# A decode-attention kernel whose output weights partly travel by five DMA engines: 320 instead of 480 rows of `wo` on that way, the rest of the quarter five rows to a partition

## The chip, the core and the metric

The kernel runs on one core of a Trainium2 chip. The metric is the time of one execution on the device in microseconds (us). Four runs of the kernel before took 189.28, 189.11, 190.93 and 194.01 us; their median is 190.1 us. The execution that was profiled is the one of 189.28 us; its profiled span is 187.5 us, which leaves 1.8 us around the span.

## The reference, cut to what matters

Attention of 4 new tokens in each of 8 sequences against a cache of 2048 keys, with 32 query heads that share 8 key/value heads, followed by the output projection. All arrays are bf16.

```python
B, Sq, D = 8, 4, 512
Hq, Hkv, Sk, Dh = 32, 8, 2048, 128
q = (x @ wq).reshape(B, Sq, Hq, Dh)                    # wq: 512 x 4096
scores = einsum("bhqd,bhkd->bhqk", q, k) * Dh ** -0.5  # k, v repeated 4 times over heads
p = softmax(scores)
o = einsum("bhqk,bhkd->bhqd", p, v)
out = o.reshape(B, Sq, Hq * Dh) @ wo                   # wo: 4096 x 512
```

Keys and values are 32 MB (2^20 bytes each) apiece, `wq` and `wo` 4 MB apiece: 72 MB are read from HBM once, and 32 KB are written.

## The kernel before, in words

**Units.** The 8 key/value heads are taken in 4 pairs and the 8 sequences one by one, which makes 32 units. A unit has 1 MB of keys and 1 MB of values, each in one tile of 128 partitions x 8192 bytes (`load_k` L108, `load_v` L118). The main loop (L405) runs over the units: it transposes the keys of unit n on TensorE (L198), copies them from PSUM on VectorE (L200), makes the scores of unit n-1 (L261), the exponentials (L272), and, two units behind, the values product (L321). Seven key tiles and six value tiles are in rotation.

**The order of the transfers.** All loads are issued by SyncE, whose queue is in the order of the list built in L148 to L158: keys of unit 0, all of `wq`, `x`, then eight small pieces of `wo` (`wo_e`, one after each of the first units), keys and values in turn, and after the values of unit 31 the pieces `wo_n` and `wo_m`. The other three quarters of `wo` follow at the end of the list (L430 to L435) in eight transfers: four of 512 KB and four of 256 KB.

**The first quarter of `wo`.** The first 1024 rows of `wo` belong to head pair 0. They are split three ways by the constants in L51:

```python
NE, WE, WM = 40, 12, 4
assert NE * WE + 128 * WM + 32 == HP * 128
```

- `wo_e`: 40 partitions with 12 rows each, 480 rows. It is loaded by `load_wo_e` (L128) in eight transfers of 5 partitions, 12,288 bytes to a partition. Since a transfer has five partitions, five DMA engines carry it, one partition each.
- `wo_m`: 128 partitions with 4 rows each, 512 rows, in one transfer of 4096 bytes to a partition (L137).
- `wo_n`: 32 partitions with 1 row each, the last 32 rows, in one transfer (L136).

The attention output must lie in the same row order to be multiplied with these pieces. `to_tokens` (L341) transposes the output of the pair to tokens and copies it to `nat_sb` (L355, L356, L359), where gaps are filled with other columns so that 64 partitions can be treated alike; the memset of `wo_e` (L173) has made the unused partitions zero. `to_wo_rows` (L361) transposes it into one slice for each row index (L376, L379, L380) and copies the slices to `oE`, `oM`, `oN` (L381 to L383).

**The projection.** `project` (L385) multiplies one slice with one row set, in two halves of 256 columns, and adds into the PSUM tile `out_ps`. Rows of `wo_e` are used after units 14 to 17, three for each (L439); `wo_m` and `wo_n` after unit 30 (L441); the other three quarters at the end (L445 to L451), pair 3 in the steps in which its 256 KB pieces arrive. Then ScalarE copies the result (L453), and two transfers write it out.

**SyncE's queue.** A transfer is issued only when the one eight places before it has landed (the queue waits show it), so at most eight are under way. The 16 DMA engines each take their share of every transfer in that order.

Of the kernel before, what the change touches and what calls it, by code (L numbers as in the profile page):

```python
# [8 lines left out]
BF16 = mybir.dt.bfloat16  # L9
# [5 lines left out]
def kernel(  # L15
# [9 lines left out]
    nc = tc.nc  # L25

    B, Sq, D = x.shape
# [4 lines left out]
    T = B * Sq  # L32
# [7 lines left out]
    HP = 2 * rep  # L40
# [7 lines left out]
    DH = D // 2  # L48


    NE, WE, WM = 40, 12, 4  # L51
    assert NE * WE + 128 * WM + 32 == HP * 128
    AX = mybir.AxisListType.X
    ADD = mybir.AluOpType.add
    assert Dh == 128 and C == 32 and NQ == 32 and G2 == 4
# [1 line left out]
    const = ctx.enter_context(tc.tile_pool(name="const", bufs=1))  # L57
# [15 lines left out]

    pad0 = const.tile([128, 192], BF16, name="pad0")
    wo_e = const.tile([64, WE, D], BF16, name="wo_e")
    wo_n = const.tile([32, D], BF16, name="wo_n")
    wo_m = const.tile([128, WM, D], BF16, name="wo_m")
    x_sb = const.tile([T, D], BF16, name="x_sb")
    wq_sb = wpool.tile([128, R, HqDh], BF16, tag="w", name="wq_sb")
# [9 lines left out]
    oT = [const.tile([128, HP, len(ps), B, Sq], BF16, name=f"oT{ps[0]}") for ps in groups]  # L89
    out_sb = const.tile([2 * T, DH], BF16, name="out_sb")  # L90
    oP12 = const.tile([128, WR, 2, T], BF16, name="oP12")
    nat_sb = const.tile([2 * T, HP * 128 + 288], BF16, name="nat_sb")
    oP3 = const.tile([128, WR, T], BF16, name="oP3")
    oP = [None, oP12[:, :, 0, :], oP12[:, :, 1, :], oP3[:, :, :]]
    oE = const.tile([64, WE, T], BF16, name="oE")
    oM = const.tile([128, WM, T], BF16, name="oM")
    oN = const.tile([32, T], BF16, name="oN")
    ident = const.tile([128, 128], BF16, name="ident")
    by_q = const.tile([128, HQ], FP32, name="by_q")
    ones = const.tile([128, 128], FP32, name="ones")  # L100
    pad = const.tile([128, 160], BF16, name="pad")
    probs = [const.tile([128, C, 2, HQ], BF16, name=f"probs{i}") for i in range(3)]

    units = [(p, b) for p in range(G2) for b in range(B)]
# [28 lines left out]
        nc.sync.dma_start(wo_e[a : a + 17 : 4, :, :], rows[b : b + 17 : 4, :, :])  # L133

    def load_wo_m():
        nc.sync.dma_start(wo_n[:, :], wo[HP * 128 - 32 : HP * 128, :])  # L136
        nc.sync.dma_start(  # L137
            wo_m[:, :, :], wo[NE * WE : HP * 128 - 32, :].rearrange("(q r) j -> q r j", r=WM)
        )

    def load_wo(p, r0, n):
        rows = wo[p * HP * 128 : (p + 1) * HP * 128, :].rearrange("(q r) j -> q r j", r=WR)
        nc.sync.dma_start(wo_sb[:, p - 1, r0 : r0 + n, :], rows[:, r0 : r0 + n, :])
# [34 lines left out]
    for e in range(2):  # L178
        for g in range(2):
            nc.vector.tensor_copy(  # L180
                out=pick[:, e, g, :], in_=ident[:, :].rearrange("d (k e) -> d e k", e=2)[:, e, :]
            )
    nc.vector.memset(q_bd[:, :, :, :, :, :, :], 0.0)
    for t in probs:
# [3 lines left out]
        out=by_q[:, :], in_=ident4[:, :].rearrange("p (c q) -> p q c", q=HQ), axis=AX, op=ADD  # L188
# [4 lines left out]
    def transpose_part(u, t):  # L193
        kp = psum_k.tile([128, JT, 128], FP32, tag="k", name="kp")
        k4 = ks[u][:, :, :].rearrange("s c d -> s (c d)").bitcast(FP32)
        for j in range(JT):
            w = (t * JT + j) * 128
            nc.tensor.transpose(kp[:, j, :], k4[:, w : w + 128], ident4[:, :])  # L198
        k_t = ktpool.tile([128, JT, 128, 2], BF16, tag="kt", name="kt")
        nc.vector.tensor_copy(  # L200
            out=k_t[:, :, :, :].rearrange("k j s e -> k (j s e)"),
            in_=kp[:, :, :].rearrange("k j s -> k (j s)").bitcast(BF16),
        )
        kt[(u, t)] = k_t
# [9 lines left out]
    for p in range(G2):  # L214
        psq = (psum_t.tile([128, HP, T], FP32, tag="t", name="psq")
               if p % 2 else psum_s.tile([128, HP, T], FP32, tag="s", name="psq"))
        for h in range(HP):
# [10 lines left out]
            out=qT_all[:, p, :, :, :],  # L228
            in_=psq[:, :, :].rearrange("d h (b s) -> d b h s", b=B),
            mul=scale,  # L230
        )
    for pp in range(0, G2, 2):
        for e in range(2):
# [9 lines left out]
            for g in range(2):  # L243
                rows = slice(g * 64, (g + 1) * 64)
                (nc.scalar.copy if g else nc.vector.tensor_copy)(  # L245
                    out=q_bd[rows, pp : pp + 2, e, :, :, g, :].rearrange("d p b g q -> d p (b g) q"),
                    in_=pse[rows, :, :, :, :].rearrange("d p b g q -> d p (b g) q"),
# [68 lines left out]
    def values(u):  # L316
        pr = probs[u % len(probs)]
        o_ps = psum_o.tile([128, NQ], FP32, tag="o", name="o_ps")
        for i in range(C):
            j, t, c = i // 8, i // 2 % 4, i % 2  # L320
            nc.tensor.matmul(  # L321
                o_ps[:, :],
                lhsT=vs[u][:, 2 * (t * JT + j) + c, :],
                rhs=pr[:, i, :, :].rearrange("s g q -> s (g q)"),
                start=(i == 0),
                stop=(i == C - 1),
            )
        o_pss[u] = o_ps
# [10 lines left out]
    nats = {}  # L339

    def to_tokens(n):  # L341
        rows = len(groups[n]) * T
        nat = psum_l.tile([rows, HP, 128], BF16, tag="l", name="nat")
        for h in range(HP):
            nc.tensor.transpose(
                nat[:, h, :], oT[n][:, h, :, :, :].rearrange("d p b s -> d (p b s)"), ident[:, :]
            )
        flat = nat[:, :, :].rearrange("t h d -> t (h d)")
        nats[n] = nat_sb[:rows, : HP * 128 + (n == 0) * 288]
        if n > 0:  # L350
            nc.vector.tensor_copy(out=nats[n][:, :], in_=flat)
            return

        w = 32 * WE
        nc.vector.tensor_copy(out=nats[0][:, :w], in_=flat[:, :w])  # L355
        nc.vector.tensor_copy(  # L356
            out=nats[0][:, w : 2 * w], in_=flat[:, NE // 2 * WE : NE // 2 * WE + w]
        )
        nc.vector.tensor_copy(out=nats[0][:, 2 * w :], in_=flat[:, NE * WE :])  # L359

    def to_wo_rows(n):  # L361
        rows = len(groups[n]) * T
        if n > 0:
            perm = psum_l.tile([128, WR, rows], BF16, tag="l", name="perm")
            by_row = nats[n][:, :].rearrange("t (q r) -> t r q", r=WR)
            for r in range(WR):
                nc.tensor.transpose(perm[:, r, :], by_row[:, r, :], ident[:rows, :rows])
            to = oP3[:, :, :] if n == 2 else oP12[:, :, :, :].rearrange("q r p t -> q r (p t)")
            nc.vector.tensor_copy(out=to, in_=perm[:, :, :])
            return  # L370

        perm = psum_l.tile([128, WE + WM + 1, T], BF16, tag="l", name="perm")
        w = 64 * WE
        by_row = nats[0][:, :w].rearrange("t (q r) -> t r q", r=WE)
        for r in range(WE):
            nc.tensor.transpose(perm[:64, r, :], by_row[:, r, :], ident[:T, :T])  # L376
        by_row = nats[0][:, w : w + 128 * WM].rearrange("t (q r) -> t r q", r=WM)
        for r in range(WM):
            nc.tensor.transpose(perm[:, WE + r, :], by_row[:, r, :], ident[:T, :T])  # L379
        nc.tensor.transpose(perm[:32, WE + WM, :], nats[0][:, w + 128 * WM :], ident[:T, :T])  # L380
        nc.vector.tensor_copy(out=oN[:, :], in_=perm[:32, WE + WM, :])  # L381
        nc.vector.tensor_copy(out=oE[:, :, :], in_=perm[:64, :WE, :])
        nc.vector.tensor_copy(out=oM[:, :, :], in_=perm[:, WE : WE + WM, :])  # L383

    def project(p, r0, n):  # L385

        for r in range(r0, r0 + n):
            if p > 0:
                o, w = oP[p][:, r], wo_sb[:, p - 1, r]
            elif r < WE:  # L390
                o, w = oE[:, r, :], wo_e[:, r]
            elif r < WE + WM:
                o, w = oM[:, r - WE, :], wo_m[:, r - WE]
            else:
                o, w = oN[:, :], wo_n
            for half in range(2):
                nc.tensor.matmul(  # L397
                    out_ps[half * T : (half + 1) * T, :],
                    lhsT=o,
                    rhs=w[:, half * DH : (half + 1) * DH],  # L400
                    start=(p == 0 and r == 0),
                    stop=(p == G2 - 1 and r == WR - 1),
                )

    for n in range(NU + A):  # L405
        w = n - A
        for t in range(2):
            if 0 < n < NU:
                transpose_part(n, t)
        if 0 <= n - 1 < NU:  # L410
            scores(n - 1)
        for t in range(2, 4):
            if 0 < n < NU:
                transpose_part(n, t)
        if w >= 0:
            p, b = units[w]
            if p in (1, 3) and b == 1:
                to_tokens(p // 2)
            values(w)
            if p in (1, 3) and b == 2:  # L420
                to_wo_rows(p // 2)
            if w % 2 == 0:
                norms(w)
            finish(w)
        if 0 <= n - 1 < NU:
            probs_to_keys(n - 1)
        load_ready(min(n + 1, NU), max(w + 1, 0))
        if w == NU - 1 - VB:
            assert not loads
            load_wo(1, 0, 4)  # L430
            load_wo(1, 4, 4)
            load_wo(2, 0, 4)
            load_wo(2, 4, 4)
            for r in range(0, WR, 2):
                load_wo(3, r, 2)  # L435

        if w == 13:
            out_ps = psum_e.tile([2 * T, DH], FP32, tag="e", name="out_ps")
        if 14 <= w < 18:  # L439
            project(0, (w - 14) * 3, 3)  # L440
        if w == NU - 2:  # L441
            project(0, WE, WM + 1)

# [42 lines left out]
```

The softmax here doesn't subtract the row's maximum and nothing guards it: scores larger than these inputs give would overflow.

## Time and profile before

| what | value |
|---|---|
| four runs, us | 189.28, 189.11, 190.93, 194.01 |
| the profiled execution, us | 189.28 |
| its span, us | 187.5 |
| TensorE busy in the span | 145.2 us, 77% |
| VectorE busy | 108.8 us, 58% |
| ScalarE busy | 69.4 us, 37% |
| GpSimd busy | 6.3 us, 3% |
| read from HBM | 75.53 MB (10^6 bytes), 403 GB/s over the span |
| packets of SyncE's DMA queue | 10,880, 96.2% of the time of 16 engines |

How to read the profile: engines are PE (TensorE), PEld (its weight loads), DVE (VectorE), ACT (ScalarE), POOL (GpSimd) and SP (SyncE); a q after the name is the engine's instruction queue. L12 is line 12 of the kernel. A group row has the line, engine and operation, the tiles written and read, the count, then busy microseconds and the mean nanoseconds of one, then the idle time before the group and what ended it. A row of the chain of waits has start, length, and what the end of the execution was waiting for in that stretch. Beside its rows, the trace holds a record for each packet that a DMA engine moved: start, duration, bytes and queue, though not the number of the engine.

### The profile page before, as it was taken

How to read it: one execution, taken by the hardware profiler on the slowest of the kernel's cores; microseconds unless marked ns; L12 is line 12 of the kernel's file. 1: busy time of each engine (PE TensorE's matmuls, PEld its weight loads, DVE VectorE, ACT ScalarE, POOL GpSimd, SP SyncE). 2: the span in 40 equal slices, each digit the busy share in tenths (PEclk: the TensorE clock that was granted, in tenths of full speed). 3: DMA queues.
4: the chain of work that ended last, by engine and by line, in shares of the span. 5: the costliest groups of instructions: out<-in, count | busy, mean ns of one | idle time of the engine just before them, and what ended most of it. 6: DMA issues, size and time to landing. Idle time of an engine off the chain costs nothing.

```text
span 187.5 us, 5654 instructions
## 1 busy us (share of the span) xinstructions
PE 145.2 (77%) x2483; PEld 120.4 (64%) x2483; DVE 108.8 (58%) x217; ACT 69.4 (37%) x202; POOL 6.3 (3%) x9
## 2 busy tenths in 40 slices
PE   0536799978669988899998998877787888888592
PEld 0516488757557777788776777665566677676371
DVE  0580598765616767557775665757375766665220
ACT  2001564461423544144545252434333343545200
POOL 8400000000000000000000000000000000000000
PEclk9999999999978999969999999999999999999879
DMA  5998999999999999999999999999999999999970
GB/s 206 465 447 376 426 430 420 429 426 426 417 435 416 425 427 430 414 430 432 416 423 430 427 418 430 427 425 420 428 420 425 428 421 427 427 425 416 400 279 13
DMA packets 10952, 75.92 MB, mean 405 GB/s; under 512 B 1288, under 2 KB 1416, under 8 KB 2568
## 3 DMA queue, kind: packets, MB, share of 16 engines
q1 hardware_dynamic: 10880, 75.55, 96.2%
q8 instruction: 19, 0.31, 0.6%
q14 instruction: 5, 0.04, 0.1%
q10 hardware_dynamic: 48, 0.02, 0.0%
HBM read 75.53 MB, written 0.03 MB: 403 GB/s over the span
## 4 chain that ended last, share of the span: by engine, by line
DMA 96%; PE 1%; SPq 0%; issue 0%; ACT 0%
DMA k_sb<-in_k_cache_dram 58%; DMA v_sb<-in_v_cache_dram 17%; DMA wo_m<-in_wo_dram 9%; DMA wq_sb<-in_wq_dram 8%; DMA wo_sb<-in_wo_dram 4%; PE kp L198 1%; SPq L113 0%; PE s_ps L261 0%; PE out_ps L397 0%; ACT out_sb L453 0%
## 5 line engine op out<-in xcount | busy, mean ns | idle before, releaser
L200 DVE COPY kt<-kp 128x1024 bf16<-128x1024 bf16 x128 | 82.5, 685 | 38.4 <-PE kp L198 38.2
L198 PE MATMUL kp<-ident,k_sb 128*128 128x128 f32 x512 | 72.6, 287 | 24.7 <-DMA k_sb<-in_k_cache_dram 15.5
L198 PEld LDWEIGHTS kp<-ident,k_sb 128*128 128x128 f32 x512 | 57.9, 146 | 36.5 <-issue 18.4
L286 ACT COPY probs<-pt 64x512 bf16<-64x512 bf16 x64 | 37.1, 579 | 54.3 <-PE pt L280 53.9
L272 ACT ACTIVATE s_sb<-s_ps 128x256 bf16<-128x256 f32 x64 | 23.9, 379 | 33.7 <-PE s_ps L261 21.6
L321 PE MATMUL o_ps<-probs,v_sb 128*128 128x32 bf16 x1024 | 30.8, 177 | 2.0 <-DMA v_sb<-in_v_cache_dram 2.0
L321 PEld LDWEIGHTS <-v_sb 128*128 128x128 bf16 x1024 | 29.9, 96 | 3.5 <-DMA v_sb<-in_v_cache_dram 2.8
L261 PE MATMUL s_ps<-kt,q_bd 128*32 128x256 bf16 x512 | 21.2, 286 | 0.0
L261 PEld LDWEIGHTS <-q_bd 128*32 128x32 bf16 x512 | 10.8, 96 | 6.2 <-issue 5.4
L311 DVE RECIPROCAL r_sb<-l_ps 128x64 f32<-128x64 f32 x16 | 8.9, 558 | 8.6 <-PE l_ps L303 8.6
L272 ACT ACTIVATION_READ_ACCUMULATOR s_sb<-s_ps 128x1 f32 x64 | 12.7, 198 | 0.0
L280 PE MATMUL pt<-ident,s_sb 128*128 128x128 bf16 x128 | 12.3, 218 | 0.0
L303 PE MATMUL l_ps<-by_gq,ones 128*128 128x64 f32 x32 | 6.9, 297 | 5.5 <-DVE by_gq L296 5.3
L332 DVE TENSOR_TENSOR oT<-o_ps,r_sb 128x32 bf16<-128x32 f32 x32 | 6.1, 191 | 5.7 <-PE o_ps L321 5.0
L303 PEld LDWEIGHTS l_ps<-by_gq,ones 128*128 128x128 f32 x32 | 4.8, 188 | 7.0 <-DVE by_gq L296 5.3
L280 PEld LDWEIGHTS <-s_sb 128*128 128x128 bf16 x128 | 8.8, 104 | 0.2 <-ACT s_sb L272 0.2
L227 ACT ACTIVATE qT_all<-psq 128x256 bf16<-128x256 f32 x4 | 1.5, 383 | 16.6 <-PE psq L220 16.6
L173 POOL MEMSET wo_e<- 64x6144 bf16 x1 | 5.2, 5212 | 0.3 <-POOLq L470 0.3
L245 DVE CAST q_bd<-pse 64x512 bf16<-64x512 f32 x4 | 2.6, 678 | 4.5 <-PE pse L236 4.5
L296 DVE TENSOR_TENSOR by_gq<-l_sb,by_q 128x64 f32<-128x64 f32 x16 | 3.4, 215 | 2.1 <-ACT s_sb L272 2.1
L180 DVE COPY pick<-ident 128x64 bf16<-128x64 bf16 x4 | 0.6, 219 | 6.5 <-POOL ident masks.py:199 6.5
L397 PE MATMUL out_ps<-wo_sb,oP 128*32 128x256 bf16 x48 | 4.0, 295 | 0.5 <-DMA wo_sb<-in_wo_dram 0.5
(45 smaller groups left out, 40.1 us busy)
## 6 DMA issues: line engine op xcount, KB each, us to landing
k_sb<-in_k_cache_dram SPq DMA_DIRECT2D x32, 1024.0 KB, 19.5
v_sb<-in_v_cache_dram SPq DMA_DIRECT2D x32, 1024.0 KB, 13.2
wq_sb<-in_wq_dram SPq DMA_DIRECT2D x1, 4096.0 KB
wo_sb<-in_wo_dram SPq DMA_DIRECT2D x4, 512.0 KB
wo_sb<-in_wo_dram SPq DMA_DIRECT2D x4, 256.0 KB, 7.7
wo_m<-in_wo_dram SPq DMA_DIRECT2D x1, 512.0 KB
wo_e<-in_wo_dram SPq DMA_DIRECT2D x8, 60.0 KB
x_sb<-in_x_dram SPq DMA_DIRECT2D x1, 32.0 KB, 13.9
```

The costliest lines, as they stand in the source:

```text
L173: nc.gpsimd.memset(wo_e[:, :, :], 0.0)
L198: nc.tensor.transpose(kp[:, j, :], k4[:, w : w + 128], ident4[:, :])
L200: nc.vector.tensor_copy(out=k_t[:, :, :, :].rearrange("k j s e -> k (j s e)"), in_=kp[:, :, :].rearrange("k j s -> k (j s)").bitcast(BF16),)
L261: nc.tensor.matmul(s_ps[t * 32 : (t + 1) * 32, :, g, :], lhsT=q_bd[:, p, e, b, g, :, :], rhs=kt[(u, t)][:, :, g * 64 : (g + 1) * 64, e], s ...
L272: nc.scalar.activation(out=s_sb[:, :, g, :], in_=s_ps[:, :, g, :], func=EXP, accum_out=l_sbs[u][:, u % 2, g : g + 1])
L280: nc.tensor.transpose(pt[:, j, :], s_sbs[u][:, j, :, :].rearrange("q g s -> q (g s)"), ident[:, :])
L286: nc.scalar.copy(out=pr[rows, :, g, :], in_=pt[rows, :, :].rearrange("s j (c q) -> s (j c) q", q=HQ),)
L303: nc.tensor.matmul(l_ps[:, :, :].rearrange("d u q -> d (u q)"), lhsT=ones[:, :], rhs=by_gq[:, :, :, :].rearrange("k u g q -> k (u g q)"), ...
L311: nc.vector.reciprocal(r_sb[:, :, :], l_ps[:, :, :])
L321: nc.tensor.matmul(o_ps[:, :], lhsT=vs[u][:, 2 * (t * JT + j) + c, :], rhs=pr[:, i, :, :].rearrange("s g q -> s (g q)"), start=(i == 0), s ...
L332: nc.vector.tensor_tensor(out=oT[(p + 1) // 2][:, :, (p == 2) * 1, b, :], in0=o_pss[u][:, :].rearrange("d (h s) -> d h s", h=HP), in1=r_sb ...
L397: nc.tensor.matmul(out_ps[half * T : (half + 1) * T, :], lhsT=o, rhs=w[:, half * DH : (half + 1) * DH], start=(p == 0 and r == 0), stop=(p ...
```

## The change

The constants become 40 partitions with 8 rows (320 rows) for `wo_e`, 128 partitions with 5 rows (640 rows) for `wo_m`, and 64 partitions with one row for `wo_n`. All that depends on them follows: transfer sizes, the columns of `nat_sb`, the slices of `oE`, `oM`, `oN`, two rows instead of three for each of units 14 to 17 in the projection, and six row sets instead of five after unit 30 (the line of the call stays as it is, since it counts by WM). The filler tile `pad` shrinks by 128 bytes to a partition.

```diff
-    NE, WE, WM = 40, 12, 4
-    assert NE * WE + 128 * WM + 32 == HP * 128
+    NE, WE, WM, WN = 40, 8, 5, 64
+    assert NE * WE + 128 * WM + WN == HP * 128
...
-    wo_n = const.tile([32, D], BF16, name="wo_n")
+    wo_n = const.tile([WN, D], BF16, name="wo_n")
...
-    nat_sb = const.tile([2 * T, HP * 128 + 288], BF16, name="nat_sb")
+    nat_sb = const.tile([2 * T, HP * 128 + 24 * WE], BF16, name="nat_sb")
...
-    oN = const.tile([32, T], BF16, name="oN")
+    oN = const.tile([WN, T], BF16, name="oN")
...
-    pad = const.tile([128, 160], BF16, name="pad")
+    pad = const.tile([128, 96], BF16, name="pad")
...
-        nc.sync.dma_start(wo_n[:, :], wo[HP * 128 - 32 : HP * 128, :])
+        nc.sync.dma_start(wo_n[:, :], wo[HP * 128 - WN : HP * 128, :])
         nc.sync.dma_start(
-            wo_m[:, :, :], wo[NE * WE : HP * 128 - 32, :].rearrange("(q r) j -> q r j", r=WM)
+            wo_m[:, :, :], wo[NE * WE : HP * 128 - WN, :].rearrange("(q r) j -> q r j", r=WM)
         )
...
-        nats[n] = nat_sb[:rows, : HP * 128 + (n == 0) * 288]
+        nats[n] = nat_sb[:rows, : HP * 128 + (n == 0) * 24 * WE]
...
-        nc.tensor.transpose(perm[:32, WE + WM, :], nats[0][:, w + 128 * WM :], ident[:T, :T])
-        nc.vector.tensor_copy(out=oN[:, :], in_=perm[:32, WE + WM, :])
+        nc.tensor.transpose(perm[:WN, WE + WM, :], nats[0][:, w + 128 * WM :], ident[:T, :T])
+        nc.vector.tensor_copy(out=oN[:, :], in_=perm[:WN, WE + WM, :])
...
         if 14 <= w < 18:
-            project(0, (w - 14) * 3, 3)
+            project(0, (w - 14) * 2, 2)
```

## The prediction

> **What bounds the kernel now.** I read the page's chain of waits first, then its DMA slices, then the chain in order of time and the timeline of the end, and last the single DMA packets.
>
> ```profile
> DMA 96%; PE 1%; SPq 0%; issue 0%; ACT 0%
> ...
> DMA  5998999999999999999999999999999999999970
> ...
> q1 hardware_dynamic: 10880, 75.55, 96.2%
> q8 instruction: 19, 0.31, 0.6%
> q14 instruction: 5, 0.04, 0.1%
> ```
>
> 96% of the chain is waiting for transfers, and the engines that carry them stand at nine tenths or more from the second slice to the 38th. Two smaller queues share them: 19 and 5 fetches of instructions. The end of the chain, start and length in us:
>
> ```profile
> 160.30 16.23 DMA wo_m<-in_wo_dram
> 176.53 0.02 issue
> 176.55 7.44 DMA wo_sb<-in_wo_dram
> 183.99 0.04 issue
> 184.04 0.41 PE out_ps L397 x4
> 184.44 0.02 issue
> 184.47 0.37 ACT out_sb L453
> ```
>
> The last piece of `wo` lands at 183.99; four matmuls, a copy and the output transfers follow, 3.5 us that the change doesn't touch. TensorE is ready for that piece:
>
> ```profile
> 181.25 1.92 PE L397 MATMUL out_ps<-wo_sb,oP 128*32 128x256 bf16 x32
> 183.40 0.40 PE L397 MATMUL out_ps<-wo_sb,oP 128*32 128x256 bf16 x4 [0.22 <-DMA wo_sb<-in_wo_dram]
> 184.04 0.40 PE L397 MATMUL out_ps<-wo_sb,oP 128*32 128x256 bf16 x4 [0.24 <-DMA wo_sb<-in_wo_dram]
> ```
>
> So the end is set by the DMA engine that finishes its share last, and the change moves bytes between engines. I split the packet records by engine: a packet starts 3 to 4 ns before the end of the one before it, so the 16 chains can be followed through; each engine must show the known order of sizes. Start to start, a packet of 8192 bytes takes 306 ns, 12,288 bytes 456 ns, 4096 bytes 155 ns, 1024 bytes 42 ns. From 4 us to the last transfers, where only the early engines wait, there is no hole in any chain, so an engine's end is the sum of its packets. The last packet of each engine ends at (us from the span's start; record time less 10.77):
>
> ```
> engines                                        end of the last packet
> 3, no instruction fetch                        178.72 179.05 179.32
> 5, two fetches of 16 KB (q8) each              180.91 181.21 181.23 181.30 181.30
> 3, three such fetches                          182.69 182.78 182.80
> 5, the eight wo_e packets                      182.03 182.05 182.60 183.17 183.72
> ```
>
> A 16 KB fetch delays its engine by 1.42 us. The five `wo_e` engines get none, but the 8 KB fetches (q14) fall on them: none, none, one, two, two, some 0.55 to 0.9 us each, in the order of their ends. The last, 183.72, is the landing at 183.99 less 0.27 us for the signal.
>
> **The change part by part.**
>
> *`wo_e` shrinks.* On each of five engines eight packets go from 12,288 to 8192 bytes: 8 x (306 - 456) = -1.20 us.
>
> Here a rule of the Trainium skill speaks against the change. "DMA: Bandwidth & Descriptors", section "Bandwidth", says that transfers under 64 KB are dominated by descriptor cost. Each `wo_e` transfer is 60 KB and becomes 40 KB. Were its time on an engine fixed, the five would gain nothing and only take on what follows below: end +0.39 us. The row says otherwise: 456 against 306 ns, half again the bytes for half again the time. A transfer's fixed latency is hidden because each engine has the next packet queued. I take -1.20; the fixed case stays as a bound.
>
> *`wo_m` and `wo_n` grow, on all 16 engines.* No 5120-byte packet is in the trace; between 155 ns (4096) and 306 (8192) the line gives 193. Eight of them: +0.30 us. If such a packet were cut into 4096 + 1024 it would take 197 ns, +0.34; I take 0.30, the line having held from 1024 to 12,288 bytes. `wo_n` has four packets of 1024 to an engine instead of two: +0.08. Together +0.39 (rounded up). Bytes balance: 5 x 32,768 taken away, 16 x 10,240 added.
>
> *Sum by engine.* The five: -1.20 + 0.39 = -0.82, so 181.21, 181.23, 181.78, 182.35, 182.90. The eleven: +0.39, so the three with three fetches end at 183.07, 183.17, 183.19. The last end goes from 183.72 to 183.19: **-0.53 us**. The gain is not 0.82, because another group of engines, 0.92 behind now and carrying 0.39 more then, becomes the last.
>
> *The same a little earlier.* `wo_m` is waited for by TensorE, in order, before the last two values products:
>
> ```profile
> 176.58 0.70 PE L397 MATMUL out_ps<-wo_m,oM 128*32 128x256 bf16 x8 [2.08 <-DMA wo_m<-in_wo_dram]
> ```
>
> Its last share ends at 176.15 now, on the engine that ends last. Then: that engine 175.33, the second 174.77, the three-fetch group (175.22 at most) 175.61; so it lands 0.54 us earlier. Two more matmuls of `wo_m` follow at about 0.08 us each (8 in 0.63 to the start of the next): TensorE goes on 0.38 us earlier than now and ends its 32 matmuls at 182.79, against a piece before the last that would land at 183.40 - 0.53 = 182.87. The cover is thin, 0.08 us. If it goes, those four matmuls start later, but 0.24 us of slack remain before the last piece, so the end holds.
>
> *TensorE and VectorE in the middle, hidden.* At 77 us four transposes of 259 ns go and one of 184 comes, and 8 matmuls of `wo_e` fewer of 0.08 us each go between 97 and 112 us: about -1.5 us at most. VectorE's copies keep their number; 384, 384, 544 columns become 256, 256, 704, within 0.1 us of the same sum by their rows (335, 335, 419 ns). TensorE waits there for keys again and again, so both are worth nothing; if TensorE were the bound they would be a gain, never a loss.
>
> ```profile
> L198 PE MATMUL kp<-ident,k_sb 128*128 128x128 f32 x512 | 72.6, 287 | 24.7 <-DMA k_sb<-in_k_cache_dram 15.5
> ```
>
> *The start.* GpSimd's memset goes from 5.21 to some 3.47 us (two thirds of the columns), and the first `wo_e` transfer waits for it:
>
> ```profile
> SPq L133 <- POOL ident masks.py:197: 4.5, 1, 4.5
> SPq L113 <- DMA wq_sb<-in_wq_dram: 5.6, 1, 5.6
> ```
>
> Behind it in SyncE's queue stand the next keys and values, so all are issued 1.7 us earlier. But `wq` keeps the 16 engines full until 14.7 us, and the queue is then stopped by the limit of eight transfers, until `wq` lands. So nothing is gained; with this cover gone it would be a gain of up to 1.7 us. The number and order of transfers, and so SyncE's waits, stay.
>
> *Instruction fetches.* 19 fetches of 16 KB to TensorE's 4966 instructions (2483 matmuls, as many loads) are 261 instructions to a fetch; the new program has 18 fewer (nine matmuls with their loads), so about 19 fetches remain, in the same rotation over eight engines.
>
> **The sum.** -0.53 us: span 187.0, and the profiled execution 189.28 becomes 188.75. The median of the four runs shown is 0.8 above the profiled one; two runs lie at 189.1 to 189.3, two above. The same median would become 189.6. I forecast 189.2, between the two, a change of -0.3% against like runs. About 1% is what a measurement of this kernel can tell from no change, given runs that differ by as much.
>
> **Rivals.**
>
> *The eleven are the ones that count: slower.* Place: the three-fetch engines; price: +0.39 us. This decides if the q14 fetches fall elsewhere in other runs, or cost less: the `wo_e` engines must be ahead of the others by less than 0.39 us, not by the 0.92 of the trace. Without any q14 fetch all five would end near 182.04, the last engine now would be at 182.80 and then at 183.19. For: five irregular fetches make up the whole lead. Against: by the same measure five fetches of 8 KB are some 650 instructions, an estimate, and ScalarE and VectorE show 202 and 217 besides those that are not counted as busy, so they belong to the program. Time: 189.3 + 0.4 = 189.7, or 190.5 on the median. Fixed cost for `wo_e` would end here too.
>
> *No change: the bytes are shared.* If the limit were HBM and not each engine, moving bytes would change nothing: 189.3 (190.1). For: 414 to 435 GB/s in nearly every slice, as if capped. Against: packets keep 306 ns when the early engines fall idle near the end, and engines end 5 us apart.
>
> *A fourth fetch.* If the shorter program moved the rotation so that one engine gets a fourth fetch, it would end at 183.19 + 1.42 = 184.61: +0.9 us, 190.2. For: the last fetch comes at 177.6, on a group that has two and then three. Against: the count stays 19.
>
> *The whole of the start.* If a hole at the start were filled by the earlier issue: up to -1.7 us more, 187.0. Against: no hole in the chains after 4 us.
>
> **How the numbers follow.** Forecast 0.60; the eleven, with fixed cost, 0.20; no change 0.10; a fourth fetch 0.06; the start 0.04. The forecast's own range is 188.4 to 190.0: 188.75 with the 0.3 us by which single costs can be off, up to 189.6 for the median and as much above. Over all, 188.2 to 191.0: the slower cases on the median are 190.5 and 191.0; below, the forecast at its best. No case but the start moves the time by 1%, so within 1% holds nearly all: the forecast, the eleven and no change give 0.90, of which the spread of the runs (one lies 0.8% above the fastest two, one 2.6%) takes 0.03 to faster and slower each; the rest follows the last two cases. Faster 0.06, within 1% 0.87, slower 0.07.
>
> **What would show it right or wrong.** In the new trace: packets of 5120 bytes near 193 ns; the `wo_e` packets near 306; the last packet of all on a three-fetch engine, the five at least 0.2 us ahead of it; `wo_m` landing half a microsecond earlier; the last landing near 183.5; TensorE still waiting for the last two pieces. Wrong would be: a `wo_e` engine still last, holes in the chains, 20 fetches, or a TensorE that no longer waits at the end.

## The result, and the profile after

| what | before | after |
|---|---|---|
| median, us | 190.33 (64 runs) | 190.23 (43 runs) |
| lowest run, us | 189.11 | 188.74 |
| the profiled execution, us | 189.28 | 189.43 |
| its span, us | 187.5 | 187.7 |
| last packet of `wo` ends, us on the prediction's zero | 183.72 | 183.57 |
| `wo_m` landed | 176.53 | 176.42 |

Ratio of the changed kernel to the one before: 0.9977, 95% interval 0.9959 to 0.9996. That is 0.44 us less (0.08 to 0.78): a small gain, under the 1% that the prediction gave as the least a measurement can tell. The ratio is the better measure than the two medians, since the runs of one kernel spread from 189 to 194 us and more. Twelve of the 64 executions before and 13 of the 43 after took more than 1.5% longer than the fastest of their kernel; the ratios and all medians further down leave such executions out (the medians here become 190.0 and 189.4), and of e1, e5 and e6, which were profiled in one, only the times are used. Ends of packets, here as in the prediction, count from a zero 0.05 us ahead of the profile's first instruction, in each run given.

The forecast was 189.2 us; the median came 1.0 higher. In size, the sum of -0.53 us lies inside the interval. That is in part luck: the profile shows something at work that the forecast named and dismissed. The end of the chain of waits after (start, length in us, what was waited for):

```profile
159.15 17.27 DMA wo_m<-in_wo_dram
176.42 0.04 issue
176.46 1.58 PE out_ps L397 x12
178.04 0.98 PE o_ps L321 x32
...
181.79 2.81 PE out_ps L397 x38
...
184.63 0.36 ACT out_sb L453
```

Before, the chain went from `wo_m` straight to a wait for `wo_sb` that lasted to 183.99. Now it never comes back to a transfer: but for 0.2 us of VectorE, TensorE works through from 176.46 to 184.60, and the output copy waits for TensorE. In this pair of executions the last packet ends 0.15 us earlier than before, and TensorE 0.16 us later (184.60 against 184.44). The page's shares say the same, DMA down from 96 to 92%, PE up from 1 to 6%:

```profile
DMA 92%; PE 6%; SPq 0%; issue 0%; ACT 0%; DVE 0%
...
q8 instruction: 19, 0.31, 0.6%
q14 instruction: 5, 0.04, 0.1%
```

The counts of fetches are unchanged, so the fourth fetch did not come. Why TensorE is busy to the end stands in the windows. Columns: window, length, busy us and count of PE, PEld, DVE, ACT and POOL, then the granted clock (1.00 is full rate), the DMA share and GB/s. First before, then after:

```profile
174.00:176.00 2.00, 0.50 (x6) 0.42 (x7) 0.75 (x2) 1.16 (x2) 0.00 (x0) 1.00 1.02 409
176.00:178.00 2.00, 1.42 (x27) 0.90 (x27) 0.00 (x0) 0.00 (x0) 0.00 (x0) 0.74 1.03 400
178.00:180.00 2.00, 1.72 (x36) 1.61 (x33) 0.27 (x2) 0.00 (x0) 0.00 (x0) 0.50 0.89 347
180.00:182.00 2.00, 1.97 (x28) 1.46 (x26) 0.89 (x2) 0.00 (x0) 0.00 (x0) 0.91 0.70 270
182.00:184.00 2.00, 1.57 (x26) 1.13 (x23) 0.00 (x0) 0.00 (x0) 0.00 (x0) 1.00 0.17 65
```

```profile
174.00:176.00 2.00, 0.00 (x0) 0.00 (x0) 0.16 (x1) 0.76 (x2) 0.00 (x0) 0.99 1.02 386
176.00:178.00 2.00, 1.54 (x13) 0.80 (x13) 0.00 (x0) 0.00 (x0) 0.00 (x0) 0.50 1.04 420
178.00:180.00 2.00, 1.72 (x43) 1.61 (x42) 0.19 (x1) 0.00 (x0) 0.00 (x0) 0.50 0.93 370
180.00:182.00 2.00, 2.00 (x24) 1.43 (x22) 0.85 (x2) 0.00 (x0) 0.00 (x0) 0.50 0.76 283
182.00:184.00 2.00, 2.00 (x34) 1.65 (x32) 0.12 (x1) 0.00 (x0) 0.00 (x0) 0.80 0.20 75
```

The clock column is the one to read: TensorE's clock is halved about the end of the wait for `wo_m`, and in the changed kernel it stays so for longer. Before, it is back at 0.91 between 180 and 182; after, still at 0.50 there, and at 0.80 in the window behind it. The timeline tells what that does to the last projection and how long the idle time was:

```profile
173.18 0.39 PE L280 MATMUL pt<-ident,s_sb 128*128 128x128 bf16 x4
176.46 1.25 PE L397 MATMUL out_ps<-wo_m,oM 128*32 128x256 bf16 x10 [2.90 <-DMA wo_m<-in_wo_dram]
...
181.72 2.86 PE L397 MATMUL out_ps<-wo_sb,oP 128*32 128x256 bf16 x40
```

Before, the four transposes ahead of this wait started at 174.11, and the wait lasted 2.08 us. They moved 0.93 us forward, because values land earlier once five engines have less to carry; `wo_m` moved forward by only 0.11. So the idle time grew by 0.8 us to 2.90. The last 40 matmuls then run without a single wait for a piece; the marks `<-DMA wo_sb` are gone. Here a rule of the Trainium skill bears on the row: "TensorE: Matmul & The Clock Gate", Part 1, has the rate drop to half after at least one idle window of about 3.4 us. By it, 2.90 us, and 2.08 before, would be harmless. The rows show 0.50 after 2.90 us, and half rate for a part after 2.08; the measurement decides. The granted clock of the traces in finer windows shows half-rate stretches of 3.41 us or a whole multiple of it: 176.97 to 180.38 before, 175.96 to 182.79 after. A second profile of the changed kernel (e8), with the same wait, has three such steps, 174.84 to 185.08:

```profile
176.38 1.25 PE L397 MATMUL out_ps<-wo_m,oM 128*32 128x256 bf16 x10 [2.91 <-DMA wo_m<-in_wo_dram]
...
181.63 4.02 PE L397 MATMUL out_ps<-wo_sb,oP 128*32 128x256 bf16 x40
```

### The profile page after: what moved, and what is told of

It reads as the page before. It is cut to its first block, busy times and chain, and to the rows that moved or that the text cites. A ratio compares the mean times of both kernels' runs of the same rounds, so it can differ in the third digit from the quotient of the medians.

```text
span 187.7 us, 5636 instructions
## 1 busy us (share of the span) xinstructions
PE 143.5 (76%) x2474; PEld 119.0 (63%) x2474; DVE 108.5 (58%) x217; ACT 69.4 (37%) x202; POOL 4.6 (2%) x9
## 4 chain that ended last, share of the span: by engine, by line
DMA 92%; PE 6%; SPq 0%; issue 0%; ACT 0%; DVE 0%
DMA k_sb<-in_k_cache_dram 47%; DMA v_sb<-in_v_cache_dram 28%; DMA wo_m<-in_wo_dram 9%; DMA wq_sb<-in_wq_dram 8%; PE out_ps L397 3%; PE kp L198 1%; PE o_ps L321 1%; PE nat L345 0%; SPq L113 0%; PE perm L367 0%; PE s_ps L261 0%; ACT out_sb L453 0%; DVE oT L332 0%; SPq L123 0%
## 5 line engine op out<-in xcount | busy, mean ns | idle before, releaser
L198 PE MATMUL kp<-ident,k_sb 128*128 128x128 f32 x512 | 71.3, 284 | 24.2 <-DMA k_sb<-in_k_cache_dram 22.6
L198 PEld LDWEIGHTS kp<-ident,k_sb 128*128 128x128 f32 x512 | 56.9, 144 | 35.9 <-issue 18.5
```

## Experiments

Two theories. *Clock* (T1 in the expectations): in the changed kernel TensorE's last stretch at half clock sets the end, and hides part of what the transfers gained. *Transfers* (T2): the last DMA engine sets it in both kernels, and the bytes are simply shared out less well than summed. A third came up on the way, *placement* of the tiles in SBUF. All ratios are to the kernel before, with 95% intervals.

### Later use of wo_m (e1, e2): no help

```diff
-        if w == NU - 2:
-            project(0, WE, WM + 1)
...
     project(1, 0, 4)
     to_wo_rows(2)
+    project(0, WE, WM + 1)
```

e1 is this in the changed kernel, e2 in the one before.

> The changed kernel, with the matmuls of wo_m and wo_n moved from before the last values product to the tail, behind the first four rows of head pair 1 (nothing else). Theory T1 (TensorE sets the end of the changed kernel: it waits 2.9 us for wo_m in order, its clock falls to half, and its 40 last matmuls end at 184.6, 0.7 us after the last landing at 183.84): TensorE waits for the last pieces again, the last matmuls end about 0.4 us after the last landing, near 184.3; ratio to the kernel before 0.995 to 0.997, better than the changed kernel's 0.9977. Rival T2 (the last DMA engine sets the end of both): the same ratio as the changed kernel, 0.997 to 0.998, and no difference in the gap between landing and last matmul.

> The kernel before, with the same move of the wo_m and wo_n matmuls to the tail. Here TensorE waited 0.22 and 0.24 us for the last two pieces, so under both theories the DMA engines set the end: ratio 0.999 to 1.001, last matmuls still about 0.4 us after the last landing near 184.0. A gain of 0.2% or more would say that TensorE's tail costs the kernel before in many runs, though not in the profiled one.

e1: 0.9996 [0.9963, 1.0029]; e2: 0.9987 [0.9954, 1.0021]. Neither differs from the kernel before within its interval: e1 met neither theory's number, and my expectation of e2's tail failed. In e2's profile the wait for `wo_m` is gone, but the clock falls all the same and ten more matmuls now stand in the slow stretch:

```profile
179.62 1.04 PE L397 MATMUL out_ps<-wo_m,oM 128*32 128x256 bf16 x8
180.59 0.39 PE L397 MATMUL out_ps<-wo_n,oN 32*32 32x256 bf16 x2
180.91 4.05 PE L397 MATMUL out_ps<-wo_sb,oP 128*32 128x256 bf16 x40
```

So TensorE sets the end of this version of the old kernel, too. What follows: taking the wait for `wo_m` away does not take the half clock away; the clock itself has to be tested.

### One part of the change, or twice the change (e3 to e6), and the pad line (e7, e8)

e3 shrinks `wo_e` alone, so that 160 rows of `wo` are left out and its output is incomplete (first diff, the constants only; loads and copies then end at row NR); e4 gives the five engines 640 rows, 160 more than before where the change gives 160 fewer (second):

```diff
-    NE, WE, WM, WN = 40, 8, 5, 64
-    assert NE * WE + 128 * WM + WN == HP * 128
+    NE, WE, WM, WN = 40, 8, 4, 32
+    NR = NE * WE + 128 * WM + WN
...
```

```diff
-    NE, WE, WM, WN = 40, 8, 5, 64
+    NE, WE, WM, WN = 40, 16, 2, 128
...
-            project(0, (w - 14) * 2, 2)
+            project(0, (w - 14) * 4, 4)
```

> Only the first half of the change: wo_e has 8 rows to a partition, wo_m stays at 4 rows and wo_n at 32; the last 160 rows of the first quarter of wo are neither loaded nor multiplied, so their part of the output is left out. By the sum of the prediction the five engines end 1.20 us earlier (at most 182.52) and the eleven as before (182.80): last landing 0.92 us earlier, ratio 0.995, if TensorE keeps up. If TensorE's tail (T1) sets the end, the gain is smaller, -0.2 to -0.6 us, ratio 0.997 to 0.999. If a wo_e transfer costs a fixed time (rival), no gain: 1.000.

> The change in the other direction: 640 rows by the five engines (16 to a partition), wo_m 2 rows to a partition, wo_n 128 rows. The five carry 8 packets of 16,384 bytes, +1.20 us, and -0.39 us from the smaller common pieces: last end 183.72 + 0.82 = 184.5. Under the sum of the prediction the ratio is 1.004 (+0.8 us), the wo_e engines last by far. If bytes are shared by all engines or the wo_e transfers cost a fixed time: 1.000 or less.

e3: 1.0062 [1.0040, 1.0083]; e4: 1.0143 [1.0105, 1.0180]. Both missed, e3 even by its sign: with less to load it took longer. The middle of the kernel shows where, in the window from 60 to 120 us. First after, then e3:

```profile
60.00:120.00 60.00, 51.93 (x921) 43.33 (x914) 40.00 (x82) 25.02 (x77) 0.00 (x0) 1.00 1.01 425
```

```profile
60.00:120.00 60.00, 50.90 (x887) 42.17 (x885) 39.16 (x81) 24.73 (x74) 0.00 (x0) 1.00 1.01 419
```

The engines are as full, the clock is the same, but 419 GB/s instead of 425 flow, though nothing was changed there. In the packet records, 99.2% of the 8192-byte packets take 309 ns after (the records overlap by 3 ns, so 306 from start to start); in e3 34% do, most of the others 312 to 321, and in e4 10%. What both share is where the big tiles lie: before and after, `wq`, the keys, the values and `wo_sb` start at multiples of 512 bytes within a partition; in e3 they are 128 bytes off, in e4 192. So the same two were built again with the filler tile sized to bring the tiles back (e5 is e3 with 32 columns, e6 is e4 with 256), and the changed kernel with the filler left as it was before (e7, below):

```diff
-    pad = const.tile([128, 96], BF16, name="pad")
+    pad = const.tile([128, 160], BF16, name="pad")
```

> The same as the kernel with only wo_e shrunk (160 rows of wo neither loaded nor multiplied, their part of the output left out), with the filler pad at 32 elements instead of 96, so that wq, keys, values and the later quarters of wo lie again at multiples of 512 bytes in SBUF, as in the kernel before; in the earlier run they lay 128 bytes off, and its packets of 8192 bytes took 312 to 318 ns instead of 309. If the placement was what made that run 0.6% slower: packets back at 309, the five wo_e engines 1.2 us earlier, last landing 0.5 to 0.9 us earlier than the kernel before, ratio 0.995 to 0.9975. If shrinking the wo_e transfers is itself harmful: again 1.004 or more.

> 640 rows by the five engines as before, with pad at 256 elements, so that the tiles lie at multiples of 512 bytes again (192 bytes off in the earlier run). If placement cost the earlier run about 1%: ratio 1.003 to 1.006 now (+0.8 us by the sum of the prediction, the five wo_e engines last). If the five engines cost more than the sum says: 1.012 and more.

> The changed kernel with one line of the change undone: pad stays at 160 elements. Nothing else moves but the place of the tiles behind it, by 128 bytes. If the placement matters: 8192-byte packets 312 to 318 ns, ratio to the kernel before 1.004 to 1.008 instead of 0.998. If not: 0.998.

> The changed kernel once more, beside the others on this chip: ratio 0.996 to 1.000. In its profile, by T1 (TensorE sets the end after a long wait for wo_m at half clock) the last matmuls run on without a wait for the last pieces of wo; by T2 (the last DMA engine sets it) they wait for them and end 0.4 us after the last landing.

| run | ratio | against the same code misplaced |
|---|---|---|
| e5 | 0.9949 [0.9926, 0.9971] | e3 1.0062 [1.0040, 1.0083] |
| e6 | 1.0029 [1.0006, 1.0051] | e4 1.0143 [1.0105, 1.0180] |
| e8, the changed kernel again | 0.9978 [0.9947, 1.0009] | e7 1.0093 [1.0065, 1.0122], four runs |

Each pair differs by 1.1 to 1.2%, by one line, the size of a tile that no instruction touches. e7's middle, with only that line of the change undone:

```profile
60.00:120.00 60.00, 51.47 (x880) 42.89 (x873) 38.75 (x80) 24.03 (x73) 0.00 (x0) 0.97 1.01 419
```

Its 8192-byte packets take 309 ns in 30% of the cases and 315.6 in the mean, against 311.2 in e8 (a few that a fetch holds up lift both means). Every engine moves 512 of them for keys and values: 512 x 4.4 ns = 2.2 us. The ratios differ by 0.0115, of 190 us also 2.2. So placement is shown as a cause of its own, and the line on `pad` is a part of the change that must not be left out. The trace fits one sentence of the Trainium skill in kind: "DMA: Bandwidth & Descriptors", "How a descriptor splits into AXI transactions", has transactions begin at 256-byte boundaries, so that another start costs beats, of 32 bytes each, that carry nothing. By it, 8192 bytes that start 128 past a boundary take 260 beats instead of 256, an estimate of 4.8 ns on 306; the means differ by 4.4. The page speaks of reading; here it is the destination that is off. With 128 and 192 bytes tried, whether 256 or 512 is the boundary stays open.

With the tiles in place, the sizes follow the sum of packets. e5's ratio is -0.97 us (0.55 to 1.4 less); by my terms, shrinking alone should bring the end from 183.72 to the three-fetch engines' 182.80, -0.92. e6 is +0.55 us (0.1 to 1.0); by the same terms the five gain 8 x (606 - 456) = 1.20 us of work (606 by the line for 16,384 bytes; most records of e4 give 611, so 608 from start to start) and lose some 0.35 on the smaller common pieces, so +0.85. Less, then more bytes on the five make it faster, then slower: they do set the end.

### wo_m early (e9, e10)

```diff
-        if u == NU + 2:
+        if u == 16:
             loads.append(("m", 0))
...
-        if w == NU - 2:
+        if w == 22:
             project(0, WE, WM + 1)
```

> The changed kernel with wo_m and wo_n loaded in the middle of the stream (beside the keys of unit 16) and multiplied after unit 22, so that TensorE no longer waits for them ahead of the last values product, and the tail holds 12 matmuls less. The bytes of every DMA engine stay. T1 (the changed kernel's end is TensorE's tail at half clock, after 2.9 us of waiting for wo_m): the last matmuls wait for the last piece again and end near 184.1 or earlier; ratio 0.991 to 0.995, and the spread of the runs shrinks. T2 (the last DMA engine sets the end): 0.997 to 0.999, as the changed kernel.

> The kernel before with the same move. The profiled run of before waited for its last pieces, so T2 says 0.999 to 1.001. T1 says that many of its unprofiled runs also end in TensorE's tail: 0.994 to 0.998. With TensorE out of the way in both, the step from this kernel to the changed one with the same move is the DMA sum alone: -0.5 us, 0.003 in the ratio.

e9: 0.9973 [0.9947, 1.0000]; e10, in the kernel before: 0.9993 [0.9970, 1.0017]. Both ratios lie where the transfer theory had them, not where the clock theory did; the profiles say why. The long wait is gone, and in e9 the last packet ends at 183.09, where the three-fetch engines were forecast to end (183.07 to 183.19). But the clock is at 0.50 from 178 to 182 again, after an idle time of only 1.26 us:

```profile
176.63 1.02 PE L321 MATMUL o_ps<-probs,v_sb 128*128 128x32 bf16 x32 [1.26 <-ACT probs L286]
...
180.36 3.59 PE L397 MATMUL out_ps<-wo_sb,oP 128*32 128x256 bf16 x40
```

So the last packet, 0.48 us earlier than in the changed kernel, is hardly seen in the ratio: TensorE takes 3.59 us for these 40 matmuls, the first 32 of which take 1.96 at full clock (e13, below). In e10 it is the same, half rate from 176.39 to 183.22 after a wait of 1.26 us. The move took the wait for `wo_m` away and not the half clock.

### The clock kept up (e11, e12)

Ten matmuls of 512 columns into a PSUM tile that nobody reads, where TensorE would idle:

```diff
         if w == NU - 2:
+            dum = psum_k.tile([128, JT, 128], FP32, tag="k", name="dum")
+            for i in range(10):
+                nc.tensor.matmul(
+                    dum[:, :, :].rearrange("p j s -> p (j s)"),
+                    lhsT=ident[:, :],
+                    rhs=q_bd[:, 0, 0, :, :, :, :].rearrange("d b g h q -> d (b g h q)"),
+                    start=True,
+                    stop=True,
+                )
             project(0, WE, WM + 1)
```

> The changed kernel with ten matmuls of 512 columns, whose result nobody reads, put into TensorE's wait for wo_m, so that it doesn't idle there. If the idle wait is what lets the granted clock fall to half for the tail: clock 0.8 to 1.0 from 176 to 184 us, last matmuls wait for the last piece, ratio 0.992 to 0.996. If the clock falls for another reason: 0.998 or, by the extra work, slower.

> The same ten matmuls in the kernel before. If its runs are spread by the clock of the tail: 0.995 to 0.999 and a smaller spread; if the DMA engines alone set its end: 0.999 to 1.001.

e11, in the changed kernel: 0.9949 [0.9931, 0.9967], median 188.94. e12, in the kernel before: 0.9975 [0.9952, 0.9998], 189.29. Work that nobody needs makes the kernel before faster, and the changed one too, though there its interval still meets the 0.9959 to 0.9996 of the kernel without it. e11's windows:

```profile
176.00:178.00 2.00, 1.35 (x21) 0.81 (x20) 0.00 (x0) 0.00 (x0) 0.00 (x0) 1.00 1.02 410
178.00:180.00 2.00, 1.72 (x48) 1.44 (x43) 0.47 (x2) 0.00 (x0) 0.00 (x0) 1.00 0.97 385
180.00:182.00 2.00, 1.66 (x28) 1.46 (x28) 0.69 (x2) 0.00 (x0) 0.00 (x0) 1.00 0.85 331
```

The clock is 1.00 until 186, and the waits for the last pieces are back:

```profile
183.75 0.40 PE L397 MATMUL out_ps<-wo_sb,oP 128*32 128x256 bf16 x4 [0.26 <-DMA wo_sb<-in_wo_dram]
184.39 0.40 PE L397 MATMUL out_ps<-wo_sb,oP 128*32 128x256 bf16 x4 [0.24 <-DMA wo_sb<-in_wo_dram]
```

(In this one execution the transfers ended later, at 184.05, so the lines show who sets the end, not at what price.) The distance from the lowest run to the median is 0.3 us, where it is 0.6 in the changed kernel and in e8. That a part of the scatter was a tail with one clock or the other is my reading of it. A gain from idle work is what the clock theory says and the transfer theory does not.

### Both (e13, e14)

e9's and e11's edits together, the ten matmuls put ahead of unit 31's values. e14 is the same in the kernel before.

```diff
+            if w == NU - 1:
+                dum = psum_k.tile([128, JT, 128], FP32, tag="k", name="dum")
...
```

> The changed kernel with wo_m and wo_n loaded beside the keys of unit 16 and multiplied after unit 22, and ten matmuls of 512 columns that nobody reads ahead of the last values product, so that TensorE neither waits for wo_m nor idles before the tail. If the sum of the prediction holds once the two obstacles (slow packets of wo_m near the end, TensorE at half clock) are gone: last landing near 183.3, TensorE waiting for the last pieces at full clock, lowest runs 188.6 to 188.7, ratio 0.992 to 0.995. If -0.53 us was too large a size in any case: within 0.001 of the kernel with the warm matmuls alone, 0.995 or above.

> The same two moves in the kernel before. The step from this kernel to the changed one with the same moves is the DMA sum alone: by the prediction -0.53 us, 0.0028 in the ratio and 0.5 us in the lowest runs; if packets of 5120 bytes are slower than the line between 4096 and 8192 wherever they stand, 0.3 to 0.4 us.

e13: 0.9929 [0.9893, 0.9965], median 188.67, lowest 188.50, the lowest median of the versions with the full output. e14: 0.9968 [0.9932, 1.0004], 189.28 and 189.06. Between them lies only the change itself: -0.61 us in the median, -0.56 in the lowest run. With 11 runs each the two intervals overlap, but eight of e13's runs are below the lowest of e14. Between e11 and e12, with the clock kept up and `wo_m` still loaded late, the change is worth 0.35 us. And the profiles show it at the place where the forecast put it. First e13, then e14:

```profile
182.78 0.40 PE L397 MATMUL out_ps<-wo_sb,oP 128*32 128x256 bf16 x4 [0.24 <-DMA wo_sb<-in_wo_dram]
183.41 0.40 PE L397 MATMUL out_ps<-wo_sb,oP 128*32 128x256 bf16 x4 [0.23 <-DMA wo_sb<-in_wo_dram]
```

```profile
183.39 0.40 PE L397 MATMUL out_ps<-wo_sb,oP 128*32 128x256 bf16 x4 [0.28 <-DMA wo_sb<-in_wo_dram]
184.02 0.40 PE L397 MATMUL out_ps<-wo_sb,oP 128*32 128x256 bf16 x4 [0.24 <-DMA wo_sb<-in_wo_dram]
```

Both wait for the last two pieces, and the last wait ends 0.61 us earlier. The last packet ends at 183.09 in e13 and at 183.71 in e14. With both obstacles out of the way, the transfer sum of -0.53 holds within this scatter.

## Why the prediction was right and where it failed

**Right: which engines count and what a packet costs.** The five `wo_e` engines reach the end of unit 31's values 0.96 to 1.24 us earlier, against -1.20 by the sum, so the time of such a transfer goes with its bytes and its fixed cost is hidden. A packet of 5120 bytes, which the trace before did not hold, takes 193 ns from start to start where nothing holds it up (57 of the 128), as the line gave. The fetches stayed 19. With `wo_m` out of the way (e9, e13), a group of engines ends at 182.94 to 183.10, as forecast for the three-fetch engines.

**Failed, first: the level.** "I forecast 189.2, between the two" mixed two things: a change worked out for one profiled execution, 0.8 us under the median, and the median itself. Against like runs the change was -0.3% and is -0.23%; against the median of the runs, the number could only come out too low. The same working gives 189.6 on the four runs' median, and the later runs of the old kernel have a median of 190.3, for which it gives 189.8, still 0.4 under the measured 190.23. Against the second pair of medians in the section on the result, 190.0 and 189.4, the 189.2 is 0.2 too low. The term that failed in 189.2 is that level, not the gain.

**Failed, second: "lands 0.54 us earlier".** `wo_m` came 0.11 us earlier, and "the last end goes from 183.72 to 183.19" came out as 183.57 and, in e8, 183.49. On two `wo_e` engines that have no 8 KB fetch the records can be followed: from the last packet of unit 31's values to the engine's end it is 9.0 us before (173.1 to 182.05) and 9.8 after (171.9 to 181.66; other engines that nothing holds up take 8.9 and 9.6), where the sum gave 9.4. The mis-sized term is the packets themselves, near the end: those of 5120 bytes take 212 ns in the mean record instead of 196, the 4096-byte ones of `wo` after them 163.5 instead of 161 before. With eight and 32 of them to an engine that is 0.13 and some 0.1 us. The two together are less than the 0.3 to 0.4 that is missing; the rest isn't attributed. In e9 and e13, with `wo_m` loaded in the middle, the 4096-byte packets take 159 ns, and the 5120-byte ones still 205.

**Failed, third, and it decides the profile: "The cover is thin, 0.08 us. If it goes ... the end holds."** It went, and the end did not hold: "a TensorE that no longer waits at the end" was one of the forecast's own signs of being wrong. I had costed the loss as four matmuls that start later, 0.24 us of slack against them. What came was half the clock for most of what follows: the 40 last matmuls take 2.86 us after and 4.02 in e8, where e13's 32 take 1.96. The clock column lay open in the profile of before, 0.74 and then 0.50 in this very stretch, and I read only the starts and waits. It also shows how a gain can bring its own loss: values that land earlier and a `wo_m` that doesn't make TensorE's idle time longer.

How long the half rate lasts does not follow the length of the wait: it is 6.8 us after 1.26 (e9, e10), 3.4 after 2.08 (before), 6.8 after 2.90 and 10.2 after 2.91 (after and e8, the same kernel). What the traces show is that the clock changes in steps of 3.41 us, and where these fall. Before, the half rate began 0.39 us after the wait for `wo_m` had ended; after, 0.50 us ahead of that; in e8, 1.54 ahead. In the step before it, TensorE was busy for 1.21 us (before), 0.84 (after), 1.61 (e8), 1.82 (e9) and 2.08 (e10). In e11 to e14, with the useless matmuls, it is busy for at least 2.48 us in each step from 169 to 182 us, and there the rate stays full. So a drop in the tail came after a step with little work in it. That the profiled execution of before had one step at half rate, and so kept its waits at the end, is then in part luck: where the steps fall differs from one execution to the next. A limit can't be read off: further ahead in the trace of before, a step with 1.72 us of work (at 40.4) was followed by full rate, and one with 2.5 (at 78.0) by half. Shown by experiment is that keeping TensorE busy removes the loss.

**Missed: the pad line.** I costed it at nothing by not speaking of it. e7 says that without it the change would have been a loss of 0.9% (0.65 to 1.2).

**The rivals.** The eleven engines with nothing gained on the five: refuted by -0.6 us in e13 against e14, and by e5 and e6, in which the five are faster and slower as their bytes are. Bytes shared at the HBM: refuted by the same pair, both with the same bytes. A fourth fetch, and the gain at the start: not seen.

**Open.** Why the packets of `wo_m` are slower than their size, and those behind them when it is loaded last; how little work in a step of 3.41 us drops the clock, and how much brings it back; which boundary counts for placement.

## What to carry to other kernels

Where transfers bound a kernel, follow the queue of each DMA engine to its own end: moving bytes off the last one gains only up to the next, and the sum by packets holds (here -0.53 against -0.56 to -0.61) as long as nothing else becomes last. Read the granted clock of the tail, in more than one profile, before calling TensorE ready: a wait that moves can cost the rate of everything behind it, and a few useless matmuls in the wait can buy it back. After any change of tile sizes look where the big transfer targets lie in a partition; 128 bytes cost this kernel 1.15%, more than the change under study was worth.

## What was not expected of the hardware

- The granted clock fell to 0.50 after waits of 2.90, 2.08 and even 1.26 us, in steps of 3.41 us that lie differently in each execution, and useless matmuls of 2.1 us held it at 1.00.
- A transfer target 128 or 192 bytes off a multiple of 512 makes most 8192-byte packets take 312 to 321 ns instead of 309: 419 instead of 425 GB/s in the middle of the kernel.
- A 16 KB instruction fetch holds up its DMA engine for 1.42 us, and eight engines of the sixteen get them all.
